# Linear attention and a snake-activated MLP on one core: w_in's first columns requested by pairs of row blocks, with alpha's load, the opening and batch 1 reordered

## The chip, the cores and the metric

The kernel runs on one core of a Trainium2 chip. The metric is device time in microseconds (us) of the whole execution, the median of several runs. Of the core's engines, TensorE (PE) does the matrix products, VectorE (DVE), ScalarE (ACT) and GpSimd (POOL) the elementwise work. SyncE (SP) issues most DMA transfers; POOL issues those that cast from f32 to bf16 on the way.

## The reference

Inputs q, k and v have shape (8, 8, 576, 64): batch, heads, positions, head size. The first part is an attention that needs no position-by-position matrix; the second a two-layer product with a sine between.

```python
q_s = softmax(q, axis=-1)              # over the 64 of a head
k_s = softmax(k, axis=2)               # over the 576 positions
kv  = einsum('bhsd,bhse->bhde', k_s, v)
x   = einsum('bhsd,bhde->bhse', q_s, kv)   # then heads side by side: (4608, 512)
h   = x @ w_in                         # (4608, 2048)
g   = h + sin(alpha * h)**2 / alpha
out = g @ w_out                        # (4608, 512), f32
```

(The kernel leaves out the reference's subtraction of maxima and its 1e-9 terms.)

## The kernel before

The 4608 rows of x are cut into nine tiles t of 512. A batch has 576 rows, nine groups j of 64, so a tile is eight of the nine groups of a batch, the ninth groups being collected elsewhere. Heads go by twos: index ii takes two heads (x = 0, 1) each from both halves (e) of the positions.

**Attention of a batch b.** q, k and v are loaded into f32 buffers (`stage`, six of them; `load`, `load0`, `load_q1`, `load_kv1`). ACT exponentiates q and k (line 119) into bf16. DVE sums q's heads and takes reciprocals (`norm_q`, lines 146 to 153; for batch 0 `norm_q0`, lines 364 to 366), DVE or POOL multiplies. v is cast to bf16 with a column of ones beside each head (`cast_v0`, `cast_v1`). `kv_mm` (line 174) multiplies k by v on PE, and the ones give k's sums; `kv_norm` (184, 185) divides. q is transposed on PE for batches 0 and 1 (`q_transpose_ii`, 201), by DMA later. `attn_x` (218) multiplies kv by q into PSUM, and copies (393, 394, 405, 491) put x, transposed, into `xT`, whose four blocks of 128 features are the inner dimension of the next product. Blocks 0 and 2 come from ii = 0, blocks 1 and 3 from ii = 1.

**The MLP of a tile t.** There are 16 slots ni of 128 hidden features. `mm_h` (263) makes four products over the blocks of `xT` in the order `KO = (0, 2, 1, 3)`, into one of the PSUM buffers that `BANKS` names. `sine` (269) runs on ACT, its square (271, 273, 275) on ACT, POOL or DVE as a letter string says, and `combine` (279) on DVE writes g. `mm_o` (283) multiplies g by w_out, 64 products a tile, and `evac_o` (295, 298) copies and stores.

**What sets the order.** Every engine takes its instructions in program order; the order is written by hand.

- *Opening.* SP issues five loads of batch 0 (q, k, q, v, k halves), ACT issues alpha's (line 313, 16 rows of 128). PE transposes alpha (329), DVE copies it and takes the reciprocal (330, 331). POOL, held by a one-element copy that waits for k (340), issues the last half of v, then w_in in six column ranges (343, 344), each as two requests of 64 partitions (`load_win`, 109), then w_out's first eight blocks. `warm_up` products (351) keep PE busy until data is there. The two casts of v's second half go to DVE and ACT; ACT copies qT's second half (395) and makes a dummy sine (396), which loads the sine table. PE makes the first products of slots 0 and 1 (`mm_h` with blocks 0 and 2) between the two attention halves, those of slots 2 and 3 after.
- *Batch 1.* While tile 0's slots run, `late` (455) issues q1's first half after slot 6, blocks 8 to 13 of w_out after 8 and 10, and q1's second half with both halves of k1 and v1 (k, v, k, v) after 13. Each q1 issue waits for a one-element DVE copy (443). Then `o_quad` interleaves tile 0's 64 output products with batch 1's attention: 46 products, transposes of ii = 0, 4, kv product, 4, attention of ii = 0 (`x_half`), 2, transposes of ii = 1, kv product, 5, attention of ii = 1, the rest. `norm_q` gives ii = 0 to POOL and ii = 1 to DVE. POOL issues w_out's last two blocks when k1 has landed (469, 470). After `kv_norm(1, 0, 1)` DVE writes two elements of `q8` (496), which let SP issue the two loads of the ninth groups (497) and then batch 2's loads. After the second `x_half`, ACT exponentiates q8 and makes the dummy sine (509) ahead of tile 1.

Of the kernel before, what the change touches and what calls it, by code (L numbers as in the profile page):

```python
# [15 lines left out]
F32 = mybir.dt.float32  # L16
BF16 = mybir.dt.bfloat16
AX = mybir.ActivationFunctionType
ALU = mybir.AluOpType
# [4 lines left out]
def kernel(  # L24
# [53 lines left out]
    def src_view(t, b):  # L78
        return t[b].rearrange("(i e) (p j) d -> (e p) i (j d)", e=2, j=J)

    win_v = moe_w_in.rearrange("(c x d) n -> x d c n", x=2, c=4)
    wout_v = moe_w_out.rearrange("(no ni) d -> ni no d", ni=128)
    out_v = out.rearrange("(b p j) d -> b j p d", b=B, j=J)

# [18 lines left out]
        load("k", k, b)  # L103
        load("v", v, b)

    def load_win(c0, c1, k0=0, k1=4):
        n, kk = slice(c0, c1), slice(k0, k1)
        for x in range(2):
            nc.gpsimd.dma_start(out=win[64 * x:64 * x + 64, kk, n], in_=win_v[x][:, kk, n])  # L109

    def load_wout(n0, n1):
        nc.gpsimd.dma_start(out=wout[:, n0:n1, :], in_=wout_v[:, n0:n1, :])
# [66 lines left out]
    def kv_norm(b, i0=0, i1=2):  # L179

        kt, m = kbd[b % 2], i1 - i0
        kvr = small.tile([128, 2, 2], F32, name="kvr")[:, :, 0:m]
        src = A["kvp", b][:, :, i0 * 65:i1 * 65].rearrange("p e (ii c) -> p e ii c", ii=m)
        nc.vector.reciprocal(kvr, src[:, :, :, D])  # L184
        nc.vector.tensor_tensor(kt[:, :, i0:i1], src[:, :, :, 0:D],
                                kvr.unsqueeze(3).to_broadcast([128, 2, m, D]), op=ALU.mult)
# [11 lines left out]
    def q_transpose_ii(b, ii, j0, j1, tp):  # L198

        for j in range(j0, j1):  # L200
            nc.tensor.transpose(tp[:, j - j0], A["qn", b][:, ii, j], identb)
# [108 lines left out]

    for n, t, ii in (("q", q, 0), ("k", k, 0), ("q", q, 1), ("v", v, 0), ("k", k, 1)):
        load0(nc.sync, n, t, ii, 0, 8 if n == "q" else J)
    nc.scalar.dma_start(out=alpha_rows, in_=moe_alpha.rearrange("(no ni) -> no ni", ni=128))
    make_identity(nc, ident)
    DVE_CP(identb, ident)
    zero = singles.tile([128, 1], F32, name="zero")
# [8 lines left out]

    tp0 = ps_h[0].tile([128, 8, 128], BF16, name="tp", tag="a")
    warm = ps_h[0].tile([128, 4, 128], F32, name="warm", tag="a")
    tpa = warm[:, 0, 0:nN]
    nc.tensor.transpose(tpa, alpha_rows, ident[0:nN, 0:nN])
    DVE_CP(alpha_sb, tpa)  # L330
    nc.vector.reciprocal(inva_sb, alpha_sb)

    def cast_v0(ii, j0, j1, eng):
        vv = vb[0].rearrange("p j (i c) -> p i j c", i=4)
        eng(vv[:, 2 * ii:2 * ii + 2, j0:j1, 0:D], staged["v", 0][:, ii::2, j0:j1])
# [2 lines left out]
    GP_CP(held, staged["k", 0][:, 0, 0, 0:1])  # L340
    load0(GP, "v", v, 1, 0, 5)
    load0(GP, "v", v, 1, 5, 9)
    for c0, c1 in ((0, 256), (256, 512), (512, 768), (768, 1024), (1024, 1536), (1536, 2048)):
        load_win(c0, c1)
    for c in range(2):
        load_wout(4 * c, 4 * c + 4)

    def warm_up(n):

        for _ in range(n):  # L350
            nc.tensor.matmul(warm, identb, A["qe", 0][:, 0:4, 0:128], start=True, stop=True)
# [30 lines left out]
    warm_up(2)  # L382
    kv_mm(0, 0, ps_k, split=True)
    warm_up(1)
    kv_norm(0, 0, 1)
    tp1 = ps_l.tile([128, 8, 128], BF16, name="tp", tag="l")
    q_transpose_ii(0, 1, 0, 8, tp1)
    cast_v0(1, 0, 5, DVE_CP)
    cast_v0(1, 5, 9, ACT_CP)

    xp = [bank("b") for _ in range(2)]
    attn_x(0, 0, 0, 8, xp)
    DVE_CP(xT[:, 0, 0:MF], xp[0])
    ACT_CP(xT[:, 2, 0:MF], xp[1])
    ACT_CP(A["qT", 0][:, 1, 0:8], tp1)
    nc.scalar.activation(zero, zero, AX.Sin)
    kv_mm(0, 1, ps_k, split=True)
    kv_norm(0, 1, 2)
    for ki in range(2):
        for ni in range(2):  # L400
            mm_h(0, ni, ki, ki + 1)
    xp = [bank("l") for _ in range(2)]
    attn_x(0, 1, 0, 8, xp)
    for x in range(2):
        DVE_CP(xT[:, 2 * x + 1, 0:MF], xp[x])
    for ki in range(2):
        for ni in range(2, 4):
            mm_h(0, ni, ki, ki + 1)

    def h_slot(t, ni, sq, lag):  # L410
        hp = mm_h(t, ni, 2 if ni < (4, 1, 0)[min(t, 2)] else 0)
# [18 lines left out]
    def take(it, n=1000):  # L430
        for _ in range(n):
            if next(it, 0) == 0:
                return
# [4 lines left out]
    with ES:  # L438
        def load_q1(ii):
            if ii == 0:  # L440
                staged["q", 1] = stage.tile([128, 4, J, D], F32, name="st_q", tag="st")
            st = staged["q", 1]
            DVE_CP(st[:, ii, 0, 0:1], zero)
            nc.sync.dma_start(out=st[:, ii::2, 0:8].rearrange("p i j d -> p i (j d)"),
                              in_=src_view(q, 1)[:, ii::2, 0:8 * D])

        def load_kv1():
            for n in "kv":
                staged[n, 1] = stage.tile([128, 4, J, D], F32, name=f"st_{n}", tag="st")
            for ii in range(2):  # L450
                for n, t in (("k", k), ("v", v)):
                    nc.sync.dma_start(out=staged[n, 1][:, ii::2].rearrange("p i j d -> p i (j d)"),
                                      in_=src_view(t, 1)[:, ii::2])

        late = {6: lambda: load_q1(0), 8: lambda: load_wout(8, 12), 10: lambda: load_wout(12, 14), 13: lambda: (load_q1(1), load_kv1())}
        for ni in range(nN):
            h_slot(0, ni, "DPPAPPAPPAAPPAPD"[ni], lag)
            flush(lag, 1)
            if ni in late:
                late[ni]()  # L460
        flush(lag, 0)

        accs = [bank(kind) for kind in "bbll"]
        os = o_quad(0, accs, [DVE_CP, ACT_CP, DVE_CP, DVE_CP])
        take(os, 46)
        for ii in range(2):
            exp_half("q", 1, ii, 8)
        norm_q(1, [GP, V], 8)
        GP_CP(held, staged["k", 1][:, 0, 0, 0:1])
        load_wout(14, 16)  # L470

        def cast_v1(ii, eng):
            vv = vb[1].rearrange("p j (i c) -> p i j c", i=4)
            eng(vv[:, 2 * ii:2 * ii + 2, :, 0:D], staged["v", 1][:, ii::2])  # L474

        exp_half("k", 1, 0)
        cast_v1(0, ACT_CP)
        exp_half("k", 1, 1)
        def transpose_q1(ii):
            tp = ps_h[0].tile([128, 8, 128], BF16, name="tp", tag="a")  # L480
            q_transpose_ii(1, ii, 0, 8, tp)
            DVE_CP(q_tile(1)[:, ii, 0:8], tp)

        transpose_q1(0)
        take(os, 4)

        def x_half(ii):
            xp = [bank("a") for _ in range(2)]
            attn_x(1, ii, 0, 8, xp)
            for x in range(2):  # L490
                (ACT_CP, DVE_CP)[x](xT[:, 2 * x + ii, MF:2 * MF], xp[x])

        kv_mm(1, 0, ps_k, split=True)
        kv_norm(1, 0, 1)
        for b in range(2):
            DVE_CP(q8[:, 0, b, 0:1], zero)
            nc.sync.dma_start(out=q8[:, :, b], in_=src_view(q, b)[:, :, 8 * D:J * D])
        load_batch(2)
        cast_v1(1, DVE_CP)
        take(os, 4)  # L500
        x_half(0)
        take(os, 2)
        transpose_q1(1)
        kv_mm(1, 1, ps_k, split=True)
        kv_norm(1, 1, 2)
        take(os, 5)
        x_half(1)
        exp_to(A["qe", 1][:, J - 2:J], q8)
        nc.scalar.activation(zero, zero, AX.Sin)
        take(os)  # L510
        for ki in range(2):
            mm_h(1, 0, ki, ki + 1)
        norm_q8()
        load("q", q, 3)
        load("k", k, 3)
        load("v", v, 3)

        def late_q8(ni):
            if ni == 11:
                tp = ps_k.tile([128, 2, 2, 128], BF16, name="tp", tag="a")  # L520
                for b in range(2):
                    for ii in range(2):
                        nc.tensor.transpose(tp[:, ii, b], A["qe", 1][:, J - 2 + b, ii * 128:(ii + 1) * 128], identb)
                DVE_CP(A["qT", 1][:, :, J - 2:J], tp)
            elif ni == 15:
                xp = ps_k.tile([128, 2, 512], F32, name="xp", tag="a")
                for ii in range(2):
                    for b in range(2):
                        for e in range(2):
                            for x in range(2):  # L530
                                r, c = slice(64 * x, 64 * x + 64), (2 * ii + b) * P
                                nc.tensor.matmul(xp[64 * e:64 * e + 64, x, c:c + P], kbd[b][r, e, ii],
                                                 A["qT", 1][r, ii, J - 2 + b, e * 64:(e + 1) * 64],
                                                 start=True, stop=True)
                DVE_CP(xT[:, :, 16 * P:18 * P].rearrange("p (x i) n -> p x i n", x=2),
                       xp[:, :, 0:4 * P].rearrange("p x (i n) -> p x i n", i=2))

        for ni in range(nN):
            h_slot(1, ni, SQ[ni], lag)
            flush(lag, 1)  # L540
            late_q8(ni)
        cast_v(2, [GP_CP, GP_CP])
        flush(lag, 0)
# [149 lines left out]
```

## Time and profile before

| | us |
|---|---|
| median of 3 runs | 282.85 (282.79 to 283.14) |
| the profiled execution | 283.53 |
| its span, first to last instruction | 281.7 |
| PE, ACT, DVE, POOL busy | 268.6, 224.1, 185.4, 83.5 |
| software-issued DMA requests of w_in: 8 of 128 KB, 4 of 256 KB | landed 4.6 and 7.6 after issue (medians) |

All times of instructions below count from the start of the span of the profiled execution. An instruction is named by its engine and its line; `out<-in` are the program's names. PEld is PE's weight load, which runs beside its products. A letter q after an engine's name is its sequencer, which issues DMAs. A "wait" is the idle time of an engine ahead of an instruction, with the one that ended it. The DMA view of a stretch counts packets, by size as written, and the bytes that they moved. The chain of waits goes back from the last instruction of a stretch, at each step to what released it.

### The profile page before, as it was taken

What the parts mean: (1) busy time and instruction counts of PE and PEld (TensorE: products, weight loads), DVE (VectorE), ACT (ScalarE), POOL (GpSimd) and SP (SyncE); (2) the same over time, 40 slices, a digit from 0 to 9 for tenths busy, and PEclk for the clock granted to TensorE, in tenths of its full rate; (3) what the DMA queues carried; (4) which work ended last, traced back from release to release, by engine and by line L of the source; (5) the groups of instructions that cost most, each with busy time, mean ns of one, the idle gap of its engine ahead of it and who ended that gap; (6) DMA issues with size and microseconds to landing.
All of it is one profiled execution on the core that took longest, in us unless ns stands there. A gap on an engine that the chain in (4) does not pass through costs nothing.

```text
span 281.7 us, 4930 instructions
## 1 busy us (share of the span) xinstructions
PE 268.6 (95%) x1890; PEld 124.2 (44%) x1919; DVE 185.4 (66%) x280; ACT 224.1 (80%) x320; POOL 83.5 (30%) x80
## 2 busy tenths in 40 slices
PE   2999989999999999999999999999999999999994
PEld 1444444444444444444544444444444444444443
DVE  3868658799868767766866677567675555555412
ACT  4989466999588999899989998999877777777400
POOL 1989410777666550115003500341000000000000
PEclk9999999999999999999999999999999999999999
DMA  7999989996699129811991199125011111111143
GB/s 260 308 187 230 296 288 310 360 329 252 142 171 396 62 61 326 316 37 40 277 381 43 37 249 403 32 57 123 1 36 40 37 37 37 40 38 42 41 106 74
DMA packets 39128, 45.82 MB, mean 163 GB/s; under 512 B 17072, under 2 KB 22464, under 8 KB 39104
## 3 DMA queue, kind: packets, MB, share of 16 engines
q1 hardware_dynamic: 33360, 40.57, 46.6%
q0 software_dynamic: 5552, 4.79, 10.2%
q8 instruction: 15, 0.25, 0.3%
q10 hardware_dynamic: 192, 0.14, 0.2%
q14 instruction: 9, 0.07, 0.1%
HBM read 36.71 MB, written 9.44 MB: 164 GB/s over the span
## 4 chain that ended last, share of the span: by engine, by line
PE 85%; DMA 5%; DVE 4%; ACT 2%; issue 2%; POOL 1%; SPq 0%; ACTq 0%
PE op L283 38%; PE hp L263 37%; DMA st_v<-in_v_dram 3%; PE kvp L174 2%; PE lp L263 2%; DMA st_q<-in_q_dram 1%; POOL s L273 1%; PE op L263 1%; PE op L663 1%; ACT s L269 1%; PE hp L218 1%; PE kvp L263 1%; DVE qs L364 1%; DVE qn L366 1%; PE xp L218 1%
## 5 line engine op out<-in xcount | busy, mean ns | idle before, releaser
L279 DVE SCALAR_TENSOR_TENSOR g<-s,inva_sb,hp 128x512 bf16<-128x512 f32 x128 | 94.5, 745 | 58.8 <-ACT s L271 53.3
L263 PE MATMUL hp<-xT,win 128*128 128x512 bf16 x505 | 127.4, 379 | 0.7 <-DVE kvr L184 0.3
L283 PE MATMUL op<-wout,g 128*128 128x512 bf16 x478 | 121.0, 379 | 1.6 <-issue 1.1
L269 ACT ACTIVATE s<-hp,alpha_sb 128x512 f32<-128x512 f32 x128 | 86.2, 682 | 23.3 <-PE hp L263 21.9
L263 PEld LDWEIGHTS <-win 128*128 128x128 bf16 x576 | 55.9, 98 | 68.0 <-issue 1.7
L283 PEld LDWEIGHTS <-g 128*128 128x128 bf16 x560 | 53.2, 98 | 64.7 <-issue 2.3
L271 ACT ACTIVATE s<-s 128x512 f32<-128x512 f32 x112 | 70.5, 630 | 3.6
L273 POOL TENSOR_TENSOR s<-s 128x512 f32<-128x512 f32 x29 | 30.1, 1056 | 21.8 <-ACT s L269 21.8
L153 POOL TENSOR_TENSOR qn<-qe,qs 128x1152 bf16<-128x1152 bf16 (+1 forms) x12 | 25.1, 2111 | 34.0 <-DVE qs L147 25.3
L295 DVE COPY o<-op 128x512 f32<-128x512 f32 (+2 forms) x33 | 21.8, 660 | 10.2 <-PE op L283 7.9
L138 POOL CAST vb<-st_v 128x1152 bf16<-128x1152 f32 x12 | 14.7, 1259 | 44.7 <-DMA st_v<-in_v_dram 44.7
L119 ACT ACTIVATE qe<-st_q 128x1152 bf16<-128x1152 f32 (+2 forms) x18 | 17.7, 1024 | 6.2 <-DMA st_q<-in_q_dram 6.0
L119 ACT ACTIVATE ke<-st_k 128x1152 bf16<-128x1152 f32 x16 | 17.9, 1151 | 0.9 <-DMA st_k<-in_k_dram 0.9
L146 DVE TENSOR_REDUCE qs<-qe 128x36 f32<-128x2304 bf16 x5 | 12.8, 2551 | 8.3 <-ACT qe L119 8.3
L119 ACT ACT_TABLE_LOAD x7 | 9.0, 1283 | 1.3 <-PEq L677 1.2
L283 PE MATMUL hp<-wout,g 128*128 128x512 bf16 x31 | 8.8, 379 | 0.1
L283 PE MATMUL lp<-wout,g 128*128 128x512 bf16 x30 | 8.6, 380 | 0.2 <-issue 0.2
L174 PEld LDWEIGHTS <-ke 64*64 64x64 bf16 x576 | 5.8, 106 | 5.3 <-issue 2.1
L174 PE MATMUL kvp<-vb,ke 64*64 64x65 bf16 x576 | 6.9, 194 | 1.1 <-ACT vb L474 0.8
L263 PE MATMUL lp<-xT,win 128*128 128x512 bf16 x31 | 7.5, 379 | 0.1
L109 POOL DMA_DIRECT2D win<-in_moe_w_in_dram x12 | 7.4, 701 | 0.0
L231 DVE CAST xT<-xp 128x1024 bf16<-128x1024 f32 (+1 forms) x7 | 7.4, 1065 | 0.0
(86 smaller groups left out, 133.5 us busy)
## 6 DMA issues: line engine op xcount, KB each, us to landing
out_dram<-o SPq DMA_DIRECT2D x70, 128.0 KB, 2.4
st_q<-in_q_dram SPq DMA_DIRECT2D x6, 1152.0 KB, 6.2
st_k<-in_k_dram SPq DMA_DIRECT2D x6, 1152.0 KB, 8.6
st_v<-in_v_dram SPq DMA_DIRECT2D x6, 1152.0 KB, 11.1
st_k<-in_k_dram SPq DMA_DIRECT2D x4, 576.0 KB, 7.3
st_q<-in_q_dram SPq DMA_DIRECT2D x4, 512.0 KB, 5.9
st_v<-in_v_dram SPq DMA_DIRECT2D x3, 576.0 KB, 8.7
wout<-in_moe_w_out_dram POOLq DMA_DIRECT2D x3, 512.0 KB, 10.4
```

The costliest lines, as they stand in the source:

```text
L119: nc.scalar.activation(dst[:, :, ii * 128:(ii + 1) * 128].rearrange("p j (x d) -> p x j d", x=2), src[:, ii::2], AX.Exp)
L138: engs[ii](vv[:, 2 * ii:2 * ii + 2, :, 0:D], staged["v", b][:, ii::2])
L146: nc.vector.tensor_reduce(qs, A["qe", b].rearrange("p j (i d) -> p j i d", i=4), axis=AXL.X, op=ALU.add)
L153: engs[ii % len(engs)].tensor_tensor(qn[:, ii, 0:j1].rearrange("p j (x d) -> p j x d", x=2), qe[:, ii], part.unsqueeze(3).to_broadcast([12 ...
L174: nc.tensor.matmul(kvp[64 * x:64 * x + 64, e, ii * 65:(ii + 1) * 65], ke[r, j, h * 64:(h + 1) * 64], vt[r, j, h * 65:(h + 1) * 65], start= ...
L263: nc.tensor.matmul(hp, win[:, KO[k], ni * 128:(ni + 1) * 128], xT[:, KO[k], t * MF % NX:t * MF % NX + MF], start=(k == 0), stop=(k == 3))
L269: nc.scalar.activation(s, hp, AX.Sin, scale=alpha_sb[:, ni:ni + 1])
L271: nc.scalar.activation(s, s, AX.Square)
L273: nc.gpsimd.tensor_tensor(s, s, s, op=ALU.mult)
L279: nc.vector.scalar_tensor_tensor(G[t][:, ni], in0=s, scalar=inva_sb[:, ni:ni + 1], in1=hp, op0=ALU.mult, op1=ALU.add)
L283: nc.tensor.matmul(acc, G[t][:, ni, j * 128:(j + 1) * 128], wout[:, ni, :], start=(ni == 0), stop=(ni == nN - 1))
L295: eng(o[:, cols], acc)
```

## The change

- w_in is requested in 128 partitions, eight requests instead of twelve: row blocks 0 and 2 of columns 0 to 255, the same of 256 to 511, row blocks 1 and 3 of columns 0 to 511, then all four blocks of four ranges of 256 columns, and of the last 512.
- alpha is loaded from SP's queue, behind the five loads of batch 0. Its transpose moves on PE behind the first kv product and one more warm-up; ACT copies it, and DVE takes the reciprocal after `kv_norm(0, 1, 2)`.
- In the opening both casts of v's second half and the copy of qT's second half go to DVE, both copies of x for ii = 0 to ACT, the copies for ii = 1 to ACT and DVE, and the dummy sine behind them. The first products of slots 0 and 1 are cut 3 to 5 with those of slots 2 and 3.
- q1, k1 and v1 are all issued after slot 11.
- The output products around batch 1's attention are cut 44, 4, 2, 4, 2, 4 and the rest. q1's normalisation is all on DVE, in pieces (`q1_sums`, `q1_norm`), the second product behind `kv_norm(1, 0, 1)`. qT's first half is copied by ACT. Each cast of v1 is split between ACT (5 groups j) and POOL (4). The q8 and batch 2 loads come behind `x_half(0)` and the second cast.

The diff, without most of its unchanged lines:

```diff
@@ -78,7 +78,7 @@
-    win_v = moe_w_in.rearrange("(c x d) n -> x d c n", x=2, c=4)
+    win_v = moe_w_in.rearrange("(c p) n -> p c n", c=4)
@@ -103,10 +103,8 @@
-    def load_win(c0, c1, k0=0, k1=4):
-        n, kk = slice(c0, c1), slice(k0, k1)
-        for x in range(2):
-            nc.gpsimd.dma_start(out=win[64 * x:64 * x + 64, kk, n], in_=win_v[x][:, kk, n])
+    def load_win(c0, c1, cc=slice(0, 4)):
+        nc.gpsimd.dma_start(out=win[:, cc, c0:c1], in_=win_v[:, cc, c0:c1])
@@ -310,7 +308,7 @@
-    nc.scalar.dma_start(out=alpha_rows, in_=moe_alpha.rearrange("(no ni) -> no ni", ni=128))
+    nc.sync.dma_start(out=alpha_rows, in_=moe_alpha.rearrange("(no ni) -> no ni", ni=128))
@@ -325,10 +323,6 @@
-    tpa = warm[:, 0, 0:nN]
-    nc.tensor.transpose(tpa, alpha_rows, ident[0:nN, 0:nN])
-    DVE_CP(alpha_sb, tpa)
-    nc.vector.reciprocal(inva_sb, alpha_sb)
@@ -340,8 +334,12 @@
     GP_CP(held, staged["k", 0][:, 0, 0, 0:1])
     load0(GP, "v", v, 1, 0, 5)
     load0(GP, "v", v, 1, 5, 9)
-    for c0, c1 in ((0, 256), (256, 512), (512, 768), (768, 1024), (1024, 1536), (1536, 2048)):
-        load_win(c0, c1)
+    for c in range(2):
+        load_win(256 * c, 256 * c + 256, slice(0, 4, 2))
+    load_win(0, 512, slice(1, 4, 2))
+    for c in range(2, 6):
+        load_win(256 * c, 256 * c + 256)
+    load_win(1536, 2048)
@@ -382,30 +380,32 @@
     kv_mm(0, 0, ps_k, split=True)
     warm_up(1)
+    tpa = warm[:, 0, 0:nN]
+    nc.tensor.transpose(tpa, alpha_rows, ident[0:nN, 0:nN])
     kv_norm(0, 0, 1)
+    ACT_CP(alpha_sb, tpa)
     cast_v0(1, 0, 5, DVE_CP)
-    cast_v0(1, 5, 9, ACT_CP)
+    cast_v0(1, 5, 9, DVE_CP)
+    DVE_CP(A["qT", 0][:, 1, 0:8], tp1)
     xp = [bank("b") for _ in range(2)]
     attn_x(0, 0, 0, 8, xp)
-    DVE_CP(xT[:, 0, 0:MF], xp[0])
-    ACT_CP(xT[:, 2, 0:MF], xp[1])
-    ACT_CP(A["qT", 0][:, 1, 0:8], tp1)
-    nc.scalar.activation(zero, zero, AX.Sin)
+    for x in range(2):
+        ACT_CP(xT[:, 2 * x, 0:MF], xp[x])
     kv_mm(0, 1, ps_k, split=True)
     kv_norm(0, 1, 2)
-    for ki in range(2):
-        for ni in range(2):
-            mm_h(0, ni, ki, ki + 1)
+    nc.vector.reciprocal(inva_sb, alpha_sb)
+    for ni, ki in ((0, 0), (1, 0), (0, 1)):
+        mm_h(0, ni, ki, ki + 1)
     xp = [bank("l") for _ in range(2)]
     attn_x(0, 1, 0, 8, xp)
-        DVE_CP(xT[:, 2 * x + 1, 0:MF], xp[x])
-    for ki in range(2):
-        for ni in range(2, 4):
-            mm_h(0, ni, ki, ki + 1)
+        (ACT_CP, DVE_CP)[x](xT[:, 2 * x + 1, 0:MF], xp[x])
+    nc.scalar.activation(zero, zero, AX.Sin)
+    for ni, ki in ((1, 1), (2, 0), (2, 1), (3, 0), (3, 1)):
+        mm_h(0, ni, ki, ki + 1)
@@ -452,7 +452,7 @@
-        late = {6: lambda: load_q1(0), 8: lambda: load_wout(8, 12), 10: lambda: load_wout(12, 14), 13: lambda: (load_q1(1), load_kv1())}
+        late = {8: lambda: load_wout(8, 12), 10: lambda: load_wout(12, 14), 11: lambda: (load_q1(0), load_q1(1), load_kv1())}
@@ -462,27 +462,16 @@
         accs = [bank(kind) for kind in "bbll"]
         os = o_quad(0, accs, [DVE_CP, ACT_CP, DVE_CP, DVE_CP])
-        take(os, 46)
-        for ii in range(2):
-            exp_half("q", 1, ii, 8)
-        norm_q(1, [GP, V], 8)
-        GP_CP(held, staged["k", 1][:, 0, 0, 0:1])
-        load_wout(14, 16)
-        def cast_v1(ii, eng):
+        def cast_v1(ii):
-            eng(vv[:, 2 * ii:2 * ii + 2, :, 0:D], staged["v", 1][:, ii::2])
-        exp_half("k", 1, 0)
-        cast_v1(0, ACT_CP)
-        exp_half("k", 1, 1)
-        def transpose_q1(ii):
+            for j0, j1, eng in ((0, 5, ACT_CP), (5, 9, GP_CP)):
+                eng(vv[:, 2 * ii:2 * ii + 2, j0:j1, 0:D], staged["v", 1][:, ii::2, j0:j1])
+        def transpose_q1(ii, eng):
-            DVE_CP(q_tile(1)[:, ii, 0:8], tp)
-        transpose_q1(0)
-        take(os, 4)
+            eng(q_tile(1)[:, ii, 0:8], tp)
         def x_half(ii):
             xp = [bank("a") for _ in range(2)]
@@ -490,20 +479,48 @@
+        def q1_sums(ii):
+            part, src = qs1[:, :, 2 * ii:2 * ii + 2], qe1[:, ii]
+            nc.vector.tensor_reduce(part, src, axis=AXL.X, op=ALU.add)
+            nc.vector.reciprocal(part, part)
+        def q1_norm(ii):
+            part = qs1[:, :, 2 * ii:2 * ii + 2]
+            nc.vector.tensor_tensor(A["qn", 1][:, ii, 0:8].rearrange("p j (x d) -> p j x d", x=2), qe1[:, ii],
+                                    part.unsqueeze(3).to_broadcast([128, 8, 2, D]), op=ALU.mult)
+        take(os, 44)
+        for ii in range(2):
+            exp_half("q", 1, ii, 8)
+        qe1 = A["qe", 1][:, 0:8].rearrange("p j (ii x d) -> p ii j x d", ii=2, x=2)
+        A["qn", 1] = att1.tile([128, 2, J, 2 * D], BF16, name="qn")
+        qs1 = small.tile([128, 8, 4], F32, name="qs1")
+        GP_CP(held, staged["k", 1][:, 0, 0, 0:1])
+        load_wout(14, 16)
+        q1_sums(0)
+        q1_norm(0)
+        q1_sums(1)
+        exp_half("k", 1, 0)
+        cast_v1(0)
+        transpose_q1(0, ACT_CP)
+        exp_half("k", 1, 1)
+        take(os, 4)
         kv_mm(1, 0, ps_k, split=True)
         kv_norm(1, 0, 1)
+        q1_norm(1)
+        take(os, 2)
+        x_half(0)
+        cast_v1(1)
         for b in range(2):
             DVE_CP(q8[:, 0, b, 0:1], zero)
             nc.sync.dma_start(out=q8[:, :, b], in_=src_view(q, b)[:, :, 8 * D:J * D])
         load_batch(2)
-        cast_v1(1, DVE_CP)
         take(os, 4)
-        x_half(0)
+        transpose_q1(1, DVE_CP)
         take(os, 2)
-        transpose_q1(1)
         kv_mm(1, 1, ps_k, split=True)
         kv_norm(1, 1, 2)
-        take(os, 5)
+        take(os, 4)
```

## The prediction

> **What bounds the kernel now.** I read the page first, then the chain of waits over 0 to 64 us, then the timeline and the DMA view of the stretches that the change touches.
>
> ```profile
> span 281.7 us, 4930 instructions
> ...
> PE 268.6 (95%) x1890; PEld 124.2 (44%) x1919; DVE 185.4 (66%) x280; ACT 224.1 (80%) x320; POOL 83.5 (30%) x80
> ...
> PE   2999989999999999999999999999999999999994
> ```
>
> TensorE is 95% busy. The slices that are not full lie in the first 14 us, and in slice five (35 to 42 us). The list of PE's waits from 28 us to the end holds 0.8 us for the cast of batch 1's v and a dozen breaks of 0.2 us at most. So after the start of tile 1's first product (45.85 us) PE runs without a break, and a shift of that point passes to the end unless something else then comes late. The change can win only in the opening (0 to 28 us) and in batch 1 (28 to 46 us). In 28.0 to 45.85 PE has 64 output matmuls at 0.2155 us, two kv products of 0.36 (72 matmuls), 16 transposes (0.9 together) and four groups of attention matmuls (0.35 each): 13.8+0.75+0.9+1.4 = 16.85 of 17.85 us. At most 1.0 us of idle time is to be had there.
>
> ```profile
> 30.30 8.71 DMA st_v<-in_v_dram
> 39.01 0.02 issue
> 39.03 1.18 ACT vb L474
> 40.21 0.04 issue
> 40.25 0.48 PE kvp L174 x35
> ...
> 46.02 0.86 PE kvp L263 x4
> ```
>
> The chain of waits: batch 1's v (first half, v0 below) lands at 39.01, its cast takes 1.18, and only then kv_mm(1,0) starts; PE had been idle for 0.85. What holds v0? Its place in a full DMA stream, read in the DMA views of 12 to 15, 18 to 22, 22 to 26 and 32.5 to 39 us:
>
> ```profile
> DMA packets 1111, 0.53 MB, mean 178 GB/s; under 512 B 69, under 2 KB 1111, under 8 KB 1111
> ...
> DMA packets 849, 0.82 MB, mean 204 GB/s; under 512 B 52, under 2 KB 849, under 8 KB 849
> ...
> DMA packets 829, 0.82 MB, mean 206 GB/s; under 512 B 25, under 2 KB 829, under 8 KB 829
> ...
> DMA packets 1240, 2.62 MB, mean 403 GB/s; under 512 B 70, under 2 KB 99, under 8 KB 1239
> ```
>
> The first three count bf16 bytes written; the f32 bytes read are twice that, 356 to 412 GB/s, like the 403 of the plain loads. From 2 to 39 us the DMA engines never rest. Loads issued before v0 must go through: v0 lands at 39.0 whatever PE does.
>
> **The change, part by part.**
>
> *Opening.* alpha's load goes from ACT's queue to SP's, behind five loads. On ACT that saves an issue of 0.45 us ahead of a table load that ends at 2.5, with q's landing at 4.91 covering it; on SP nothing stood behind until 23.2. Both are worth 0. The last of these lands at 10.50; I take 10.6 for alpha, and PE reaches its transpose at 11.03, after the lone warm-up. If alpha waited for the first w_in request (12.57), PE would be 1.5 us late there; see below for what covers that. ACT copies alpha (0.2) after exp k; DVE takes the second v cast (0.6) and the copy of qT (0.69, its time in batch 1; it was 1.02 on ACT). Then kv_norm(0,1) ends at about 13.9 against 13.65, since DVE has 0.6+0.69 before it; qT is there at 13.45 against 14.13. So attn_x(0,1), which waited for qT until 14.34, starts at 13.95. Five early products follow (1.08), and slot 0 resumes at 15.5, where it resumed at 16.13: PE gains 0.65. The Sin table load (1.28) and its dummy (0.2) now come after xT's copy (ends 14.98), so the first sine starts at 16.4 against 16.55: ACT gains only 0.15. PE's buffers were free 1.2 to 1.6 us before use, so PE keeps its gain, ending h at about 27.4 instead of 28.0.
>
> *w_in.* Twelve requests become eight (four issues of 0.6 fewer on POOL, whose queue was ahead of the stream anyway). The first request now serves the first products alone, one request (0.68 us) sooner; it landed at 12.57 and xT is ready at 12.85, so this hides. In rows of 256 columns (512 B written) go 1.25 MiB instead of 1.0 MiB: 0.26 MB at 178 instead of 204 GB/s costs 0.19; fewer closing packets win some 0.09. Net +0.1 on the stream. The last request (columns 1536 to 2047) lands at 23.7 to 23.9 (its last half landed at 23.65), and PE comes for it at 23.9 instead of 24.55: 0.2 at risk.
>
> Here the halves of 64 partitions may matter. Rows: halves with 1 KB packets ran at 204 GB/s, whole requests of w_out at 206, halves with 512 B packets at 178. So packet size and not the half explains the lower rate, and I take 178 for the new requests. No row has 512 B packets in 128 partitions; the bounds are 178 and 206, that is +0.1 to -1.0 us (1.31 MB at 206 instead of 178) for all later loads. [...]
>
> *Batch 1's loads.* q1's first half is issued after slot 11 instead of 6, the rest after 11 instead of 13 (26.9 instead of 29.4 to 31.3). The stream is full and the order before v0 (w_out to block 14, q1 twice, k0) carries the same bytes: 1.84 MB of w_out at 205 (8.95 us) and 2.23 MB of q1, k0, v0 at 405 (5.5) after w_in's end at 22.2 make 36.65, and the last engine trailed 2.4 behind. So v0 lands at 39.0 again, +0.1 from w_in, from -0.5 to +0.4 if the trailing changes. Earlier issue wins nothing. q1's first half lands later (33.7 instead of 29.9); exp, sum, reciprocal, product (1.06+1.22+0.25+1.22) give qn at 37.65 (both products on DVE now; POOL's took 1.91); PE comes at 36.9, waits 0.7, does transposes and four matmuls and is at kv_mm(1,0) by 39.0, still before v0's cast. **So the opening's 0.65 is lost in this wait**, and so would be 0.8 us of a late alpha.
>
> *Behind v0.* The cast is split: ACT 5 of 9 (0.72 by the rows 1.17 and 0.61), POOL the rest (0.6, 4/9 of 1.26 rounded up). kv_mm(1,0) at 39.78 instead of 40.25. ACT then copies qT (1.02), exponentiates k (1.16), copies xT (0.59), casts (0.72). The second transposes write the buffer that this xT copy frees, at 42.2; two matmuls, kv_mm(1,1) at 43.1 (43.26 before), four, attention, four: 2.45 later, tile 1 starts at 45.55 instead of 45.85. (The first of these four needs w_out's last blocks, issued when k0 has landed as before and landed at 43.07: 0.4 of cover.) **PE gains 0.3.**
>
> *What is late next.* The two small loads for q8, and all of load_batch(2), are issued by SP behind a DVE copy that now stands behind q1_norm(1) (1.22, waiting for kv_norm) and an xT copy (0.68).
>
> ```profile
> 41.37 0.92 SPq L497 DMA_DIRECT2D q<-in_q_dram  x2
> ```
> ```profile
> 45.79 0.73 ACT L119 ACTIVATE qe<-q 128x256 bf16<-128x256 f32 x2
> 46.53 1.28 ACT L509 ACT_TABLE_LOAD   x1
> 47.83 0.20 ACT L509 ACTIVATE zero<-zero 128x1 f32<-128x1 f32 x1
> 47.93 0.67 ACT L269 ACTIVATE s<-kvp,alpha_sb 128x512 f32<-128x512 f32 x1
> ```
>
> kv_norm ends at 40.8, q1_norm at 41.95, the copy at 42.55, the gates at 42.7: SP issues at 42.7 instead of 41.37. The second of the two landed 3.48 after the first issue (44.85), with w_out's end beside it, so now 45.6 to 46.2. ACT's xT copy ends at 45.6; exp, table and dummy then put tile 1's first sine at 47.75 to 48.35, between -0.2 and +0.4 around today's 47.93; I take +0.1. ACT and then DVE run without slack from there: DVE's last product of tile 1 ends at 63.61, and PE's sixteenth output matmul starts at 63.68 with this wait ahead of it:
>
> ```profile
> 63.66 0.33 PEld L283 LDWEIGHTS <-g 128*128 128x128 bf16 x3 [0.32 <-DVE g L279]
> ```
>
> So tile 1's end follows ACT's start, not PE's: PE's 0.3 has a cover of 0.07 only, and the sum is +0.1-0.07, about 0. Batch 2 and 3 arrive some 1.3 later; q2 landed at 48.5 for use at 62.75, v3 at 68.04 for a POOL cast whose next consumer waits until 74.1: hidden.
>
> **Sum.** The profiled execution took 283.53 (span 281.7 and 1.8 around it), 0.7 over the median 282.85. A shift of 0.0 to +0.1 gives **282.9**. "Same" means within 0.2%, or 0.57 us, about what a measurement of this kernel can tell from no change.
>
> **Rivals.**
> - *Slower: tile 1's sines start late.* q8 lands at 46.2 or later, the first sine is at 48.35, and DVE's last product 0.4 late; with v0 0.3 late by w_in's smaller packets and another trailing engine, 0.7 us: 283.5. It decides once the first sine is more than 0.6 later than 47.93. For: DVE's order puts three instructions (2.6 us with their waits) ahead of the gate, and a POOL cast took 2.29 instead of 1.17 at 68.6 beside DVE's product, as casts here may. Against: the DMA is empty by 43, so q8 may land fast. 0.30.
> - *Faster: the stream shortens.* 128-partition requests lift w_in to 206 GB/s, or the engine that trails 2.4 us trails less. v0 0.9 earlier moves the whole chain behind it, q8's gate included: 282.0. For: the two and a half microseconds of trailing have no fixed cause in the profile. Against: 204 for halves. 0.23.
> - *The change doesn't do what it says*: the opening gains and batch 1 is issued earlier, and neither shows in the end, as the DMA stream sets both. That is the forecast, 282.9: 0.47.
>
> **Range.** The slower case with both ends of its terms (+0.4, +0.4 and 0.2 of w_in's last request) reaches 283.8; the faster, -1.0 from the stream and -0.1, 281.8. The forecast's own range is 282.4 to 283.3. Chances: faster 0.23, same 0.47, slower 0.30.
>
> **What would show it.** Right: first products of tile 0 resume near 15.5, h ends near 27.4, v0 lands at 39.0, PE idle before kv_mm(1,0) is still over 1 us (in two pieces), tile 1 starts near 45.55, its first sine near 48. Wrong: v0 landing before 38.4 (the faster rival), q8's exp after 46.3 (the slower), alpha's transpose later than 12.5, or PE waits behind 64 us that before did not have.

## The result, and the profile after

The changed kernel takes 283.91 us (median of 21 runs, 282.95 to 285.19); the kernel before, on the same chips, 282.79 (21 runs, 282.50 to 283.59). The ratio is 1.0035 with a 95% interval of 1.0025 to 1.0045: the change costs 1.0 us, between 0.7 and 1.3. The forecast was 282.9, no change.

The profiled execution took 284.68, its span 282.9, against 283.53 and 281.7 before: 1.15 more, so these two executions show the difference of the medians, and their stretches can be compared one by one. The page of the changed kernel (its line numbers are shifted, by 2 in the helpers; q8's loads, L497 before, are L516):

```profile
span 282.9 us, 4924 instructions
...
PE 268.6 (95%) x1890; PEld 124.2 (44%) x1919; DVE 185.0 (65%) x278; ACT 224.7 (79%) x323; POOL 82.1 (29%) x77
...
PE   2999969989999999999999999999999999999994
```

PE's busy time is the same to a tenth, over the same number of recorded products, so the lost time is idle time of PE. Two slices are emptier: the sixth (35 to 42 us), 6 for 8, and the ninth (57 to 64 us), 8 for 9. The list of PE's waits from 28 to 66 us says what is in them (total, number and longest), before and then after:

```profile
PE kvp L174 <- ACT vb L474: 0.8, 1, 0.8
PE lp L283 <- issue: 0.2, 1, 0.2
```
```profile
PE tp L199 <- DVE qn L489: 1.9, 1, 1.9
PE tp L540 <- DVE g L277: 1.0, 1, 1.0
PE hp L216 <- DVE kbd L183: 0.3, 1, 0.3
```

The first of the changed kernel's waits stands in batch 1's attention, where the kernel before waited 0.85 for v's cast. The second is new, and lies behind tile 1's start, where the kernel before had no wait (its 0.2 of "issue" is at 40.9). To see which counts, I compared the same events in both traces, in order of time:

| us | before | after | later by |
|---|---|---|---|
| first q load lands | 4.91 | 4.34 | -0.57 |
| first product of tile 0 | 13.39 | 12.72 | -0.67 |
| first output product of tile 0 | 28.00 | 27.03 | -0.97 |
| v0 (v's first half of batch 1) lands | 39.01 | 39.25 | +0.24 |
| kv_mm(1,0), then kv_mm(1,1) | 40.25, 43.26 | 40.06, 43.47 | -0.19, +0.21 |
| tile 1's first product | 45.85 | 46.07 | +0.22 |
| q8's second load lands | 44.85 | 46.97 | +2.12 |
| first sine of tile 1 | 47.93 | 49.21 | +1.28 |
| first output product of tile 1 | 60.43 | 61.64 | +1.21 |

So the opening's gain was there and was gone at v0, as the forecast had it; 0.2 of the loss comes with v0; and 1.0 comes between tile 1's first product and its first output product. It comes from ACT. This is ACT's timeline after (start, duration, instruction, and in brackets the idle time before it and what ended it):

```profile
45.44 0.59 ACT L480 CAST xT<-hp 128x512 bf16<-128x512 f32 x1
47.07 0.72 ACT L117 ACTIVATE qe<-q 128x256 bf16<-128x256 f32 x2 [1.04 <-DMA q<-in_q_dram]
47.81 1.28 ACT L526 ACT_TABLE_LOAD   x1
49.10 0.20 ACT L526 ACTIVATE zero<-zero 128x1 f32<-128x1 f32 x1
49.21 0.67 ACT L267 ACTIVATE s<-kvp,alpha_sb 128x512 f32<-128x512 f32 x1
```

ACT stands for 1.04 us with the ninth groups of q not there; the exponential, the table load and the dummy follow without a gap, and the first sine behind them. Before, the same exponential started at 45.79 with no wait. Why the load is late is seen in DVE's and SP's timelines. First DVE before, then DVE and SP after:

```profile
40.99 0.29 DVE L185 TENSOR_TENSOR kbd<-kvp,kvr 128x128 bf16<-128x128 f32 x1
41.20 0.20 DVE L496 COPY q<-zero 128x1 f32<-128x1 f32 x2
```
```profile
40.80 0.29 DVE L183 TENSOR_TENSOR kbd<-kvp,kvr 128x128 bf16<-128x128 f32 x1
41.01 1.22 DVE L489 TENSOR_TENSOR qn<-qe,qs 128x1024 bf16<-128x1024 bf16 x1
42.15 0.68 DVE L480 CAST xT<-hp 128x512 bf16<-128x512 f32 x1
42.75 0.20 DVE L515 COPY q<-zero 128x1 f32<-128x1 f32 x2
```
```profile
42.92 0.92 SPq L516 DMA_DIRECT2D q<-in_q_dram  x2
```

The two one-element copies that release SP stand behind q's second product and a copy of x, 1.9 us of work; before, they followed `kv_norm` at once. The second load is issued at 43.38 and lands at 46.97.

PE meets the lateness at 57.6 us. These are two stretches of the chain of waits, and one row of PE's timeline:

```profile
37.52 1.09 POOL held L498
...
42.72 7.21 issue
...
54.85 2.73 DVE g L277 x4
57.58 0.04 issue
57.62 0.38 PE tp L540 x4
```
```profile
57.62 0.38 PE L540 MATMUL tp<-identb,qe 128*128 128x128 bf16 x4 [0.95 <-DVE g L277]
```

Line 540 is the transposes of the ninth groups, which the program puts into tile 1's products. They write the PSUM buffer of slot 7, which is free when DVE has combined that slot. DVE follows ACT, ACT started 1.28 late, and PE waits 0.95. The chain itself doesn't name q8: behind POOL's cast it has 7.21 us of "issue", a stretch in which it follows an engine that waited for nothing the profile shows. At a long "issue" one leaves the chain and asks each engine for its own idle time.

### The profile page after: what moved, and what is told of

The parts are those of the page before. It is cut to its first block, busy times and chain, and to the rows that moved or that the text cites. A ratio compares the mean times of both kernels' runs of the same rounds, so it can differ in the third digit from the quotient of the medians.

```text
span 282.9 us, 4924 instructions
## 1 busy us (share of the span) xinstructions
PE 268.6 (95%) x1890; PEld 124.2 (44%) x1919; DVE 185.0 (65%) x278; ACT 224.7 (79%) x323; POOL 82.1 (29%) x77
## 4 chain that ended last, share of the span: by engine, by line
PE 81%; issue 5%; DMA 5%; POOL 4%; ACT 3%; DVE 2%; SPq 0%; POOLq 0%; ACTq 0%
PE op L281 38%; PE hp L261 35%; DMA st_k<-in_k_dram 3%; POOL s L271 3%; ACT s L267 2%; DVE g L277 2%; PE kvp L172 2%; PE warm L349 2%; DMA st_q<-in_q_dram 1%; PE op L261 1%; PE op L680 1%; PE hp L216 1%; PE xp L216 1%; PE tp L199 0%; POOL vb L469 0%
## 5 line engine op out<-in xcount | busy, mean ns | idle before, releaser
L151 POOL TENSOR_TENSOR qn<-qe,qs 128x1152 bf16<-128x1152 bf16 x11 | 23.2, 2128 | 28.1 <-DVE qs L145 23.0
L349 PE MATMUL warm<-qe,identb 128*128 128x512 bf16 x10 | 4.7, 615 | 5.0 <-ACT qe L117 5.0
## 6 DMA issues: line engine op xcount, KB each, us to landing
st_v<-in_v_dram SPq DMA_DIRECT2D x3, 576.0 KB, 10.6
```

The source lines that it names most:

```text
L151: engs[ii % len(engs)].tensor_tensor(qn[:, ii, 0:j1].rearrange("p j (x d) -> p j x d", x=2), qe[:, ii], part.unsqueeze(3).to_broadcast([12 ...
```

## The experiments

Three theories could explain the 1.0 us. **Q**: q8's loads are issued late, and tile 1's first sine with them. **L**: batch 1's loads all stand behind slot 11, q1's first half lands 4.8 later (34.69 instead of 29.89), and PE waits 1.93 for it. **W**: w_in's new requests, or the opening, cost time in the stream. The kernels and their ratios to the kernel before (95% interval in brackets; each had one profiled execution among its runs):

| kernel | us | before, same chip | ratio |
|---|---|---|---|
| e1: after, q8 early | 283.38 | 282.94 | 1.0010 [0.9996, 1.0025] |
| e2: before, q8 late | 283.85 | 282.94 | 1.0034 [1.0017, 1.0051] |
| e3: before, new opening | 283.09 | 282.94 | 1.0011 [0.9993, 1.0028] |
| e4: before, new w_in requests | 283.11 | 282.94 | 1.0008 [0.9987, 1.0029] |
| e5: after, old times of batch 1's loads | 283.65 | 282.64 | 1.0030 [1.0016, 1.0045] |
| e6: e1 and e5 together | 282.72 | 282.64 | 1.0007 [0.9988, 1.0025] |
| e7: after, v0 ahead of q1's second half | 285.86 | 282.64 | 1.0105 [1.0072, 1.0138] |
| e8: after, q8 later still | 291.08 | 282.64 | 1.0308 [1.0283, 1.0332] |

### e1: the changed kernel with q8's loads where they were

```diff
         kv_norm(1, 0, 1)
+        for b in range(2):
+            DVE_CP(q8[:, 0, b, 0:1], zero)
+            nc.sync.dma_start(out=q8[:, :, b], in_=src_view(q, b)[:, :, 8 * D:J * D])
         q1_norm(1)
...
         cast_v1(1)
-        for b in range(2):
-            DVE_CP(q8[:, 0, b, 0:1], zero)
-            nc.sync.dma_start(out=q8[:, :, b], in_=src_view(q, b)[:, :, 8 * D:J * D])
         load_batch(2)
```

> The changed kernel, with only the two q8 gates and loads moved up again, to just behind kv_norm(1,0,1); batch 2's loads stay late. Theory Q (the late q8 loads delay tile 1's first sine from 47.93 to 49.21, and so everything behind): SP issues at about 41.2, q8 is there by 45, the first sine follows ACT's copy of x (ends 46.03) and comes near 48.2, and the time falls by 0.8 to 1.2 us, to 282.8 to 283.1. Theory L (batch 1's loads after slot 11 cost, since q1 comes at 34.7 and PE waits 1.93 us for its product): no change, 283.9. Theory W (the w_in requests and the opening cost): no change, 283.9.

Measured: 1.0010, where the change as it stands has 1.0035. About 0.7 of the 1.0 us is gone with three moved lines; 0.8 to 1.2 had been expected, and what is left, 0.0010, can't be told from nothing. One thing the expectation has wrong: batch 2's loads stand behind q8's on SP and move with them (q2 issued at 42.57, in the changed kernel at 43.93). The last part of this section shows that they have no share in the time. The profile of e1, ACT's timeline first and then the whole list of PE's waits from 28 to 66 us:

```profile
46.21 0.74 ACT L117 ACTIVATE qe<-q 128x256 bf16<-128x256 f32 x2
...
48.37 0.67 ACT L267 ACTIVATE s<-kvp,alpha_sb 128x512 f32<-128x512 f32 x1
```
```profile
PE tp L199 <- DVE qn L489: 2.2, 1, 2.2
```

ACT no longer waits for q8, and the wait at line 540 is gone. The wait for q1's product is still there, longer even; it costs 0.2 at tile 1's start in this execution (the last table of this section). So that wait, the largest in the changed kernel's list, is not the one that matters.

### e2: the kernel before with q8's loads late

```diff
         kv_norm(1, 0, 1)
+        cast_v1(1, DVE_CP)
+        take(os, 4)
+        x_half(0)
         for b in range(2):
...
         load_batch(2)
-        cast_v1(1, DVE_CP)
-        take(os, 4)
-        x_half(0)
         take(os, 2)
```

> The kernel before, with only the q8 gates, the q8 loads and batch 2's loads moved behind the first half of x and the second v cast. Theory Q: the gates come at about 43.4, q8 lands near 47, the first sine of tile 1 comes near 49.2 instead of 47.93, and the time rises by 0.8 to 1.2 us, to 283.6 to 284.0. Theories L and W: at most 0.2 us above the kernel before.

Measured: 1.0034, the whole of what the change costs, by this one move in the kernel before. PE's waits, 28 to 66 us, and the row of ACT:

```profile
PE tp L523 <- DVE g L279: 1.0, 1, 1.0
```
```profile
45.76 0.77 ACT L119 ACTIVATE qe<-q 128x256 bf16<-128x256 f32 x2 [0.88 <-DMA q<-in_q_dram]
```

The same wait of 0.95 us at the same transposes appears (line 523 in the old numbering). In its profiled execution e2's span is 281.7, that of the kernel before, since v0 landed 1.49 earlier there (37.52). That is why I don't judge single executions by their spans here, but by distances that v0's landing doesn't move, given below.

### e8: q8's loads later still

```diff
-        for b in range(2):
-            DVE_CP(q8[:, 0, b, 0:1], zero)
-            nc.sync.dma_start(out=q8[:, :, b], in_=src_view(q, b)[:, :, 8 * D:J * D])
         load_batch(2)
...
         kv_norm(1, 1, 2)
+        for b in range(2):
+            DVE_CP(q8[:, 0, b, 0:1], zero)
+            nc.sync.dma_start(out=q8[:, :, b], in_=src_view(q, b)[:, :, 8 * D:J * D])
```

> The changed kernel with the q8 gates and loads one step later still, behind kv_norm(1,1,2); batch 2's loads are now ahead of them. Theory Q: the gates come at 44.5 instead of 42.9, the q8 loads stand behind 3.5 MB of batch 2 in the DMA stream as well, tile 1's first sine comes as much later as q8 lands, and the end follows one to one: 1.6 us more if q8 overtakes batch 2, and 9 to 11 us more if it waits for it. Theories L and W: no change against the changed kernel, 283.9.

Measured: 1.0308, 8.4 us over the kernel before and some 7.3 over the changed one, between the two sizes expected. The edit did more than it was meant to: the gates had also held back batch 2's loads behind them on SP, which now go out at 29.9 to 34.7 and fill the DMA engines ahead of q8 and of w_out's last blocks (mean busy share 0.98 to 1.15 in each half microsecond from 39 to 46; in the changed kernel it is down to 0.00 at 43.0). SP and ACT, and then PE's waits (14 to 70 us):

```profile
43.69 1.56 SPq L522 DMA_DIRECT2D q<-in_q_dram  x2
```
```profile
52.56 0.72 ACT L117 ACTIVATE qe<-q 128x256 bf16<-128x256 f32 x2 [5.48 <-DMA q<-in_q_dram]
...
54.71 0.67 ACT L267 ACTIVATE s<-kvp,alpha_sb 128x512 f32<-128x512 f32 x1
```
```profile
PE kvp L261 <- DVE g L277: 2.4, 1, 2.4
PE hp L281 <- DMA wout<-in_moe_w_out_dram: 1.9, 1, 1.9
PE tp L540 <- DVE g L277: 0.9, 1, 0.9
```

Issued only 0.77 later than in the changed kernel, q8 lands 5.1 later (52.09), and the first sine is 5.5 later. It follows the landing as Q says, but as a test of size the run is spoilt: w_out's wait of 1.9 and a granted clock of 0.50 behind it (last section) are in the 8.4 too. What it shows beside Q is that two one-element copies also order all that stands behind the gated load on its queue.

### e5 and e6: the old times of batch 1's loads, without and with q8 early

```diff
-        late = {8: lambda: load_wout(8, 12), 10: lambda: load_wout(12, 14), 11: lambda: (load_q1(0), load_q1(1), load_kv1())}
+        late = {6: lambda: load_q1(0), 8: lambda: load_wout(8, 12), 10: lambda: load_wout(12, 14), 13: lambda: (load_q1(1), load_kv1())}
```

e5 is the changed kernel with this alone; e6 has e1's edit too.

> The changed kernel with batch 1's loads issued as before (q1's first half after slot 6, the rest after 13); the q8 loads stay late. Theory Q: tile 1's first sine stays 3.1 us behind tile 1's start and the distance from tile 1's start to its first output product stays 15.6 us instead of 14.6, so at least two thirds of the loss stay: 283.5 to 284.0. Theory L: q1's product is ready by 34, PE's wait of 1.9 us for it goes, and the time falls to 282.8 to 283.1.

> The changed kernel with both undone: the q8 loads up behind kv_norm(1,0,1), and batch 1's loads at the times of before. Theory Q together with a small price of L (0.3 us, where v's first half lands early and PE then waits for q1's product): 282.5 to 283.0, that is the kernel before or up to 0.4 us faster. If something else of the change costs: 283.3 or more.

Measured: e5 1.0030, no better than can be told from the 1.0035; e6 1.0007, no difference from the kernel before. Undoing L alone wins nothing that the runs can tell; undoing both restores the time. Between e1 and e6 lie 0.0003, with intervals of 0.0015 and more on each side, so whether L costs a tenth of a per cent once q8 is early stays open. PE's waits of e5, 14 to 70 us:

```profile
PE kvp L172 <- ACT vb L469: 0.8, 1, 0.8
PE tp L540 <- DVE g L277: 0.4, 1, 0.4
PE kvp L261 <- DMA win<-in_moe_w_in_dram: 0.3, 1, 0.3
```

With q1 early the wait for its product has gone, and a wait of 0.8 for v's cast stands in its place: the 1.93 us had been a wait that v0 would have imposed anyway. In the changed kernel v0 landed at 39.25 and its cast took 0.74, to 40.01; kv_mm(1,0) started at 40.06.

### e3 and e4: the opening and the w_in requests in the kernel before

e4 has only these hunks; e3 has all that the change's diff does ahead of batch 1, alpha's load and the opening's order included.

```diff
-    win_v = moe_w_in.rearrange("(c x d) n -> x d c n", x=2, c=4)
+    win_v = moe_w_in.rearrange("(c p) n -> p c n", c=4)
...
+        nc.gpsimd.dma_start(out=win[:, cc, c0:c1], in_=win_v[:, cc, c0:c1])
...
+    for c in range(2):
+        load_win(256 * c, 256 * c + 256, slice(0, 4, 2))
+    load_win(0, 512, slice(1, 4, 2))
+    for c in range(2, 6):
+        load_win(256 * c, 256 * c + 256)
+    load_win(1536, 2048)
```

> The kernel before with the whole opening of the changed one (alpha from SP, the w_in requests, the engines and the order of the first products), and batch 1 as before. Theory Q: tile 0's h ends near 27.0 instead of 28.0 and PE waits about 1.9 instead of 0.85 us for v's first half at 39.0: the time is that of the kernel before within 0.3 us. Theory W: 0.5 to 1.1 us slower. If the opening's gain did reach the end, it would be 0.6 to 1.0 us faster.

> The kernel before with only the eight w_in requests of 128 partitions. Theory Q: the same within 0.3 us, as v's first half lands at 39.0 to 39.2. Theory W: 0.5 us slower or more, w_in's last request landing later than 24.6 and PE waiting for it. By the faster rate (512 B packets at 196 instead of 178 GB/s): v lands 0.4 earlier, 0 to 0.4 us faster.

Measured: 1.0011 and 1.0008, both with 1 in their intervals. Neither w_in nor the opening costs or wins what these runs can tell (W falls, to within 0.2 to 0.3%; and e2 has the whole loss with neither). In e3's profiled execution the first output product came at 27.25, 0.75 earlier than before, and PE then waited 0.39 at kv_mm(1,0): the gain is there and ends in the wait for v0: tile 1 starts 6.84 behind v0, as before. The span of that execution was 280.5, the lowest of all, with v0 at 37.80; its median is no better than before, so it isn't a faster kernel.

### e7: v's first half ahead of q1's second

If v0 bounds batch 1, loading it earlier should help. e7 issues q1's first half after slot 6 and, after 12, k0, v0, q1's second half, k1, v1, moves q8's gates up, and q1's second half to behind the first transposes (its exponential) and behind the copy of x (its sum and product):

```diff
         kv_norm(1, 0, 1)
-        q1_norm(1)
-        take(os, 2)
-        x_half(0)
-        cast_v1(1)
         for b in range(2):
...
+        take(os, 2)
+        x_half(0)
+        q1_sums(1)
+        q1_norm(1)
+        cast_v1(1)
```

> As the kernel with early q8 loads, with batch 1's loads in another order: q1's first half after slot 6, then after slot 12 k's and v's first halves, only then q1's second half, k's and v's second; exp, sums and product of q1's second half behind x's first half. If v's place in the full DMA stream sets the first kv product, v's first half lands 1.3 us earlier (0.52 MB at 405 GB/s less ahead of it) and the first kv product starts near 38.7 instead of 40.2; but v's second half lands no earlier, so tile 1's start gains 0 to 0.8 us: 282.0 to 283.0. If not, no change against the kernel before.

Measured: 1.0105, slower by 3 us, which neither expectation had. v0 did land earlier, at 37.10, and kv_mm(1,0) started at 38.26, 1.8 earlier than in the changed kernel. But q1's second half landed at 38.34, and PE waited for its product. From PE's timeline of e7:

```profile
40.13 0.59 PE L281 MATMUL hp<-wout,g 128*128 128x512 bf16 x2
43.26 1.04 PE L199 MATMUL tp<-identb,qn 128*128 128x128 bf16 x8 [2.53 <-DVE qn L492]
...
45.72 1.89 PE L281 MATMUL hp<-wout,g 128*128 128x512 bf16 x4
```

My edit put 2.7 us of DVE work (sum, reciprocal, product) between x's copy and those transposes. And four output products behind it take 1.89, where four take 1.04 elsewhere: the granted clock had fallen to 0.50 (last section). The two runs of e7 in which it hardly fell (mean granted clock 0.997 and 1.000) took 284.28 and 284.29, so e7 is some 1.6 us slower even with the clock up. The theory that v0 bounds kv_mm(1,0) stands; that an earlier v0 shortens this kernel was not shown, and this edit, with both costs in it, can't decide it.

### What all profiled executions have in common

v0 landed anywhere from 37.52 to 39.32 in the profiled executions of kernels that issue it behind the same bytes, more than any effect sought here (38.35 to 39.32 in the three with all of batch 1's loads behind slot 11, 37.52 to 39.01 in the six with the old times). From the same traces three distances can be read that it leaves nearly alone (e7 and e8, with their other waits, are left out):

| | tile 1's first product after v0 | q8's landing after that product | first sine after that product | tile 1's first output product after it |
|---|---|---|---|---|
| before | 6.84 | -1.00 | 2.08 | 14.58 |
| e3 | 6.84 | -0.50 | 2.08 | 14.58 |
| e4 | 6.84 | -0.47 | 2.08 | 14.58 |
| e6 | 6.81 | -1.76 | 2.01 | 14.44 |
| e1 | 7.04 | -1.14 | 2.01 | 14.44 |
| e5 | 6.81 | +0.28 | 2.53 | 14.95 |
| e2 | 7.32 | +0.81 | 3.11 | 15.60 |
| after | 6.82 | +0.90 | 3.14 | 15.57 |

The first column hardly changes, whatever was done to the opening, to w_in or to batch 1's order (e1's 7.04 has the long wait for q1's product in it; in e2 v0 was so early that it no longer set the start). The others fall into two groups. Where q8 lands 0.47 or more ahead of tile 1's first product, the first sine comes 2.0 to 2.1 behind that product, and how much earlier q8 lands makes no difference. Where it lands later, the sine follows the landing by 2.24 to 2.30. So q8 has to land some 0.2 ahead of that product to be covered. Past this the last column grows as the sine does, one to one: against the kernels of the same order with q8 early (e1 and e6; before) the sine and the output product are late by 1.13 and 1.13 in the changed kernel, by 0.52 and 0.51 in e5, by 1.03 and 1.02 in e2. The account of the 1.21 in the table of the first section: 0.24 from v0's landing, 1.13 from q8, and 0.14 less, since with q8 early the new order has 14.44 for 14.58; the sum is 1.23. What follows is the same in all ten executions, e7 and e8 too: from tile 1's first output product to the end of the span 221.24 to 221.30 us. So nothing behind that product has a part in the loss, batch 2's loads included, though its q landed anywhere from 45.39 (e8) to 50.62 (the changed kernel).

## Why the prediction was wrong, and where it was right

**The failed step: the size of q8's lateness.** The mechanism was in the text, as the slower rival. The forecast's term was "I take +0.1" for tile 1's first sine, from a bracket of 45.6 to 46.2 for q8's landing. That rival's sign, the exponential of q8 after 46.3, came: it started at 47.07. q8 landed at 46.97 and the sine was 1.28 late, so the term measured 1.04, which is 1.28 less the 0.24 by which v0 moved the stretch (1.13 against the same order with q8 early). Two numbers made it too small. The gate was estimated at 42.7, and SP issued at 42.92, since kv_mm(1,0) ran at 40.06 and not at 39.78. And the landing was put at 2.9 to 3.5 after the first issue, that is around and below the only value that the trace of before had (3.48), in the hope that an emptier DMA would help. In the nine executions without batch 2's loads ahead of it, it lay between 3.12 (e6) and 4.27 (e7), and was 4.05 in the changed kernel. One measured latency is not an upper bound. Even so the rows at hand leaned to the slower side: 42.7 and 3.48 give 46.18, and ACT's rows from the exponential to the sine add 2.14, together 48.3, 0.4 late; the +0.1 was taken from the middle of a bracket that had this as its end.

**Where it reaches PE.** The prediction named the sixteenth output product with 0.07 of cover. It was right that tile 1's end follows ACT and DVE, and wrong in the place: PE stalls for 0.95 already at 57.6, at the transposes of the ninth groups, for slot 7's buffer. The changed kernel then runs on without a further wait of this kind.

**Batch 1's rearrangement.** Predicted gain of PE 0.3, tile 1 at 45.55 with v0 at 39.0, that is 6.55 behind v0. Measured 6.82, against 6.84 before: the gain was 0.02. The split cast did bring kv_mm(1,0) from 1.24 to 0.81 behind v0, as predicted (0.78); but 3.41 instead of 3.01 then lie between the two kv products, because eight output products instead of six stand between them (0.2155 each). An order that moves a wait past work that must be done anyway wins nothing.

**q1's late landing.** Predicted 33.7, and a PE wait of 0.7; it landed at 34.69 and the wait was 1.93. e1 and e5 show that this cost little, and why: v0's cast would have held kv_mm(1,0) to nearly the same moment.

**The opening: right in size, in part by luck.** The first sine of tile 0 came at 15.97 and the first output product at 27.03 (predicted 16.4 and 27.4), and the gain was lost in the wait for v0, as predicted. But the prediction read attn_x(0,1) as waiting for qT until 14.34, and took w_in's first request as hidden. In the kernel before and in e2, both with the old opening, attn_x(0,1) starts 0.95 behind tile 0's first product (13.39 and 14.34; 13.29 and 14.24), though the copy of qT ended at 14.12 in the one and at 13.68 in the other: PE's own four products came last. The first of them ran 0.14 behind the landing of the second half of w_in's first columns (13.25 and 13.15), which it needs as much as the first half. e4, with nothing new but the requests, has that landing at 12.12, the first product at 12.60 and the first output product at 27.39, against 27.91 in e2. So about half of the gain, as far as single executions tell, came from a term that the prediction put at nothing.

**w_in's stream: outside its bounds.** Predicted +0.1 to -1.0 us. The executions of the new requests whose first load was as early as e2's (4.45 to 4.54) have the last request landing at 23.17 (e3), 23.40 (e4), 23.49 (e7), 23.94 (e6) and 24.07 (e5), against 23.00 in e2 with the old ones: 0.2 to 1.1 later, and nothing of the -1.0. It cost nothing that can be told, since v0 comes last: e4's ratio is 1.0008. The 0.09 for fewer closing packets was an estimate (69 packets under 512 B from 12 to 15 us before, 36 after); no run shows its time by itself.

**Right.** That a gain of the opening ends in the wait for v0, and that an earlier issue wins nothing: loads issued 1 to 2 us earlier landed no earlier (v0 went out at 28.65 for 30.30). alpha landed at 10.17 (taken as 10.6), and its transpose ran at 10.92. v0's landing, 39.25 for 39.0 +0.1, is right too, but with a scatter of 37.52 to 39.32 that is luck.

**The range** ended at 283.8, and the result lies at that end: 283.91, or 283.84 if the ratio is applied to the 282.85 from which the forecast started. That end was made of +0.4 for the sine, +0.4 for v0 and 0.2 for w_in's last request. Measured were 1.04, 0.24 and no wait of PE for that request, so that they add up to nearly the same is luck.

## What to carry to other kernels

When an instruction that releases a DMA is moved behind other work on its engine, don't price the move by the time of the next consumer alone: take the landing as issue plus the longest latency of such a load that the traces show, with a margin if there is only one (here 3.12 to 4.27 in nine executions), subtract the moment at which the consumer is ready, and everything past that slack goes one to one into the chain (here the sine came 1.13 late, and the output product 1.13). Here a load that had 0.8 us to spare was made 2.1 later. The longest wait in the list need not be the costly one: 1.9 us before the transposes cost almost nothing, since another load would have held PE there, while 1.0 us further on, where nothing else was late, cost 1.0. And where one load's landing scatters by more than the effect, compare distances within each execution rather than spans.

## What the runs showed of the hardware beside this

**TensorE's granted clock fell to a half after some idle stretches of 1.9 to 2.5 us, and not after others.** The granted clock (the column PEclk) by stretches of e7, around its wait of 2.53 us, with PE's busy time and its instructions ahead of it:

```profile
38.60:40.70 2.10, 2.02 (x28) 1.00 1.10 297
40.70:43.20 2.50, 0.03 (x1) 0.86 1.09 242
43.20:46.00 2.80, 2.74 (x47) 0.50 1.03 400
46.00:49.00 3.00, 3.00 (x11) 0.50 1.04 409
```

It stood at a half from 42.5 to 49.3, which makes some 3 us of PE's work last twice as long; e7's six runs spread from 284.28 to 287.30. In e8 a wait of 1.91 at 43.0 was followed by half the clock from 46.2 to 49.6. In the changed kernel a wait of 1.93 and in e1 one of 2.22 left it at 1.00; in e8 the four products behind a later wait of 2.36 took 1.02, for 1.03 at a clock of 1.00 in the changed kernel and 1.89 at 0.50 in e7. The stretches at half clock lasted 3.4 us (e8) and 6.8 (e7). What decides whether the clock falls behind an idle stretch, no run here shows: its length alone doesn't, since 1.91 brought a fall and 2.22 none.

**A one-element copy on POOL took 1.09 us.** It started at 37.52 beside DVE's product of two operands in the SBUF (37.34 to 38.57) and ended with it; in the kernel before the same copy took 0.19, beside a sum over one operand (36.38 to 37.60). In e1 it took 1.06, again ending within 0.06 of DVE's product, in e8 0.59, in the other six 0.19. The two rows, of after and of before:

```profile
37.52 1.09 POOL L498 COPY held<-st_k 128x1 f32<-128x1 f32 x1 [8.22 <-DMA st_k<-in_k_dram]
```
```profile
36.69 0.19 POOL L469 COPY held<-st_k 128x1 f32<-128x1 f32 x1 [1.27 <-DMA st_k<-in_k_dram]
```

w_out's last blocks, which POOL issues behind it, so went out at 38.55 instead of 36.93, and landed at 43.28 instead of 43.07, in time. That DVE's product held the copy back is my reading of the rows of the changed kernel (1.09) and e1 (1.06); no run varies that alone.

**512-byte packets in 128 partitions.** The DMA view of the changed kernel from 12 to 15 and from 17 to 19 us:

```profile
DMA packets 810, 0.53 MB, mean 176 GB/s; under 512 B 36, under 2 KB 810, under 8 KB 810
...
DMA packets 784, 0.39 MB, mean 196 GB/s; under 512 B 18, under 2 KB 784, under 8 KB 784
```

From 17 to 19 us the new requests wrote packets of some 500 bytes at 196 GB/s; the kernel before, with packets of some 900 in halves of 64 partitions, moved 195 there. The rate of 178 that I had taken for small packets belongs to the stretch of 12 to 15 us, which both kernels pass at about that rate, and not to the size of the packet alone.
